# Cross-partition maxima moved from POOL to TensorE products in an attention, gating and feed-forward kernel with a planned instruction order

## The chip, the cores and the metric

The kernel runs on one core of a Trainium2 chip. The metric is device time in microseconds (us), the median of several executions. Five engines run their own instruction lists and meet only at semaphores: PE (TensorE, matrix products), DVE (VectorE), ACT (ScalarE), POOL (GpSimd) and SP (SyncE, which here issues nearly all the DMAs). An engine runs its list strictly in the order in which it was written, so an instruction that waits holds up all that stand behind it, and a DMA that waits in SP's list holds up every later DMA of that list.

## The reference

Three stages follow one another. Attention has 4 batches of 12 heads, with 448 positions of 64 elements:

```
q_n, k_n = rmsnorm(q, g_q), rmsnorm(k, g_k)
scores = scale * q_n @ k_n^T;  attn = softmax(scores);  x = attn @ v
```

Then come a gated block (d_model 768, d_ff 1024) and a feed-forward block with a residual:

```
h = relu(x @ w_in);  u, v = halves of h
v_s = w_spatial (over positions) @ layernorm(v) + b_spatial
x = (u * v_s) @ w_out
out = x + relu(layernorm(x) * g_ln @ w_ch1) @ w_ch2
```

All activations are float32. The weights arrive as 64-bit floats, which the kernel unpacks itself.

## The kernel before

Every large product is done in two-part half precision: a float32 operand is scaled by a power of two and split into a high and a low f16 part (`split`), and three of the four part products are added in PSUM. The scales must be the same on all 128 partitions, so for each operand a bound over all partitions is needed. Most operands get theirs in `sum_scale`: it squares, casts to bf16, multiplies by a matrix of ones on PE, which leaves the sum over partitions in every partition, and derives the power of two with a few narrow DVE instructions. Two bounds are taken in another way: for the batches 1 to 3 of `v` (`v_scale`), and for the maximum of `g_ln`. These call POOL's library routine `partition_all_reduce` with the operation max, and `v_scale` then takes a square root on POOL.

**Attention** goes in 24 pairs of heads (6 pairs to a batch). `att_load` loads q and k into a `raw` tile (4 buffers) and v into `vraw`. `att_front` computes the sums of squares for the norm: ACT squares, DVE reduces, POOL raises to the power -1/2 (`rs`, L192, two pairs at once). `att_back` multiplies `raw` by `rs` on DVE (L207), takes the high part on ACT (L209) and the low part on POOL (L210, for pair 0 on DVE), then issues a DMA transpose into `hT` (L213) and two DMA copies that exchange the halves of `hT` (L215). The scores (L247) need both. The tile `qk16` between L209 and L213 has one buffer. Softmax is L258 to L283, and the product with v is L300 to L307.

**Weights.** `moe1_weights` loads w_in (parts v and u), w_spatial and w_out. `load_weight` fetches 64-bit words into a tile `wide` (2 buffers; the tiles called `v_w`, `u_w`, `o_w` and `r_w` in the trace), and DVE puts the float32 together with three instructions (L422 to L424). The last of the three frees the buffer for the next fetch. `v_scale` fetches a batch of v in three tiles `vpre`, which share two buffers with the squares of `att_front`.

**The gated block** (`moe1`, L543 to L620) of batch b runs beside the attention of batch b+1. Its output goes to DRAM (`x2d`), is read back, normed and transposed into `xnT` (`layernorm`). **The feed-forward block** (`moe2`, L668 and L687) then takes 12 blocks of 256 hidden units, whose weights `prep_block` unpacks.

**The order.** The program is first traced in the order of the Python code, where `merge` interleaves generators: at each step it resumes the one that has used the smallest share of its total, by the numbers that the generators yield. Then `issue_order` throws that order away: `traced` collects the dependences and the rotation of tile buffers, which stays that of the trace; `schedule` runs a model of the machine with costs from `hold`, forward and backward in turns; and `SHAKES` lists how often, and with which random disturbances of the priorities. The last forward pass fixes the order of every engine's list, SP's included. So a change in any cost, in the trace order or in `SHAKES` moves instructions everywhere.

Of the kernel before, what the change touches and what calls it, by code (L numbers as in the profile page):

```python
# [20 lines left out]
P = 128  # L21
# [109 lines left out]
def v_scale(c, b):  # L131


# [16 lines left out]
    if b:  # L150
        am = c.small.tile([P, 1], F32, tag="vam", name=f"vam{b}")
        nc.gpsimd.partition_all_reduce(am[:], mx[:], channels=P, reduce_op=bass_isa.ReduceOp.max)
        nc.gpsimd.tensor_tensor(am, am, c.half, op=ALU.pow)
        c.sv[b] = c.const.tile([P, 2], F32, tag=f"sv{b}", name=f"sv{b}")
        pow2_scale(c, am[:], 14, c.sv[b][:, 0:1], c.sv[b][:, 1:2])
    else:
        nc.vector.tensor_tensor(mx, mx, mx, op=ALU.mult)
        c.sv[b] = sum_scale(c, mx, f"V{b}", pool=c.const)
# [269 lines left out]
def split_weight(c, src, k, n, parts, wide, key):  # L428

    w = c.w1pool.tile([P, 2, k, n], F16, tag=f"w_{key}", name=f"w_{key}")  # L430
    mx = c.small.tile([P, parts], F32, tag="wmx", name=f"wmx_{key}")
    kk = k // parts
    raws = []
    for j in range(parts):
        raws.append(load_weight(c, src[j * kk * P:(j + 1) * kk * P], (kk, n), wide, "wf", f"{key}{j}"))
        squares(c, raws[j], w[:, 1, j * kk:(j + 1) * kk], mx[:, j:j + 1])
        yield 0
    sc = sum_scale(c, mx, key, pool=c.const)
    for j in range(k):
        split(c, raws[j // kk][:, j % kk], w[:, 0, j], w[:, 1, j], sc[:, 0:1])  # L440
        yield 0
    c.w[key] = (w, sc)


def prep_sp(c):
# [6 lines left out]
    for j in range(2):  # L452
# [5 lines left out]
        yield 0  # L458
    sc = sum_scale(c, mx, "sp", pool=c.const)
    for t in range(NTB):  # L460
# [6 lines left out]
        yield 0  # L467
# [239 lines left out]
SHAKES = ((0, 0, 4), (1003, 1000, 3), (1005, 8000, 4), (1012, 8000, 2))  # L707
# [147 lines left out]
def schedule(g, prio, back=False):  # L855
# [18 lines left out]
    for _ in g.ops:  # L874
        best = (math.inf, 0)
        for e, l in todo.items():
            for o in l:
# [3 lines left out]
                if o.xfer > 1000:  # L881
                    s = max(s, dma_at - o.lead)
# [73 lines left out]
def kernel(ctx: ExitStack, tc: tile.TileContext, q, k, v, g_q, g_k, w_in, w_spatial, b_spatial,  # L956
# [43 lines left out]
    c.half = c.const.tile([P, 1], F32, name="half")  # L1000
    nc.vector.memset(c.half, 0.5)
# [15 lines left out]
    gm = c.small.tile([P, 1], F32, tag="gm0", name="gm0", bufs=1)  # L1017
    nc.vector.tensor_reduce(gm, c.gln, axis=AX.X, op=ALU.max, apply_absolute_value=True)
    nc.gpsimd.partition_all_reduce(c.gmax[:], gm[:], channels=P, reduce_op=bass_isa.ReduceOp.max)
    c.gmax2 = c.const.tile([P, 1], F32, name="gmax2")  # L1020
    nc.vector.tensor_tensor(c.gmax2, c.gmax, c.gmax, op=ALU.mult)
# [8 lines left out]
    merge((att(0, 7), 6 * 7000), (moe1_weights(c), 20))  # L1030
# [80 lines left out]
```

## Time and profile before

| | us |
|---|---|
| median of 3 executions (1199.38 to 1205.27) | 1202.64 |
| the profiled execution | 1199.02 |
| its span, first to last instruction | 1197.2 |
| PE busy | 1087.7 (91%) |
| DVE busy | 867.8 (72%) |
| ACT busy | 564.3 (47%) |
| POOL busy | 231.9 (19%) |

The page divides the span into 40 slices of about 30 us. In the first, PE is at 0 tenths; from about 550 us on, in the feed-forward block, it is at 9 tenths throughout. Between the two lie attention and the gated blocks. A busy share is a mean: a stage can be limited by waits that the share doesn't show, so the views that matter here are the stretches (busy time by stage) and the timelines of single engines with the idle time ahead of an instruction.

### The profile page before, as it was taken

The numbers are of one execution on the slowest core, as the hardware profiler recorded it, in microseconds if no ns is written. First come the engines' busy times: TensorE is split into PE (matmuls) and PEld (weight loads), VectorE is DVE, ScalarE is ACT, GpSimd is POOL, SyncE is SP. The second block draws the span as 40 slices with busy tenths as digits, with TensorE's granted clock in tenths as the row PEclk, the third lists the DMA queues.
The fourth block names the chain that finished last, engine by engine and source line by source line (L and its number), as shares of the span: only waits on it lengthen the run. The fifth ranks groups of instructions, "written<-read, shape, count | busy, mean of one in ns | idle before, by whom it ended". The sixth has DMA issues, their size and how long they took to land.

```text
span 1197.2 us, 17032 instructions
## 1 busy us (share of the span) xinstructions
PE 1087.7 (91%) x6385; PEld 570.2 (48%) x6385; DVE 867.8 (72%) x1712; ACT 564.3 (47%) x1088; POOL 231.9 (19%) x166
## 2 busy tenths in 40 slices
PE   0378789799979988997999999999999999999998
PEld 0234335344434434443555555555555555565555
DVE  6778799888897884985985756757584947675334
ACT  2589898678777863656223232414141332313111
POOL 3055458463573320311000000000000000000000
PEclk9989979989989998998999999999999999999999
DMA  8677798999999995888530303111121203010013
GB/s 253 183 193 176 186 204 199 184 212 195 181 206 207 173 159 157 216 199 207 206 106 1 106 1 106 46 61 39 67 75 33 87 20 106 7 48 1 1 53 132
DMA packets 231747, 149.42 MB, mean 125 GB/s; under 512 B 192816, under 2 KB 209264, under 8 KB 231664
## 3 DMA queue, kind: packets, MB, share of 16 engines
q1 hardware_dynamic: 227280, 137.32, 47.7%
q10 hardware_dynamic: 4384, 11.01, 2.7%
q8 instruction: 50, 0.82, 0.3%
q14 instruction: 33, 0.27, 0.1%
HBM read 85.45 MB, written 11.01 MB: 81 GB/s over the span
## 4 chain that ended last, share of the span: by engine, by line
PE 68%; DVE 7%; ACT 5%; DMA 4%; issue 2%; POOL 2%; ACTq 0%; SPq 0%; DVEq 0%; POOLq 0%
PE ps L668 27%; PE ps L687 26%; PE psu L564 4%; PE psv L543 2%; PE ps_o L307 2%; PE ps_s L247 2%; PE pss L577 2%; DMA x2d<-x2o 2%; DVE p L283 2%; ACT pexp L263 1%; PE pso L605 1%; DVE nb L258 1%; POOL rs L192 1%; DMA hT<-qk 1%; ACT p L282 1%
## 5 line engine op out<-in xcount | busy, mean ns | idle before, releaser
L687 PE MATMUL ps<-xnT,wt 128*128 128x384 f16 (+1 forms) x1728 | 347.0, 354 | 8.0 <-DMA xnT<-xn 8.0
L668 PE MATMUL ps<-wt,h 128*128 128x384 f16 x2016 | 344.1, 326 | 0.0
L671 DVE SCALAR_TENSOR_TENSOR x<-ps,wio,x 128x384 f32<-128x384 f32 x336 | 200.6, 614 | 131.6 <-PE ps L668 128.9
L668 PEld LDWEIGHTS <-h 128*128 128x128 f16 x2016 | 196.7, 98 | 133.7 <-issue 0.3
L687 PEld LDWEIGHTS <-wt 128*128 128x128 f16 x1728 | 168.6, 98 | 161.9 <-DMA xnT<-xn 8.5
L690 ACT ACTIVATE hf<-ps 128x512 f32<-128x512 f32 (+1 forms) x96 | 51.9, 540 | 354.1 <-PE ps L687 338.4
L247 PE MATMUL ps_s<-hT 128*64 128x448 f16 x672 | 100.4, 385 | 33.4 <-ACT pexp L263 25.7
L263 ACT ACTIVATE pexp<-ps_s,nb 128x448 f32<-128x448 f32 x168 | 105.5, 639 | 25.9 <-DVE nb L258 22.8
L692 DVE TENSOR_TENSOR h<-hf,h 128x512 f16<-128x512 f32 (+1 forms) x96 | 59.5, 620 | 62.6 <-ACT h L691 62.1
L258 DVE TENSOR_REDUCE nb<-ps_s 128x2 f32<-128x896 f32 x96 | 91.8, 966 | 17.5 <-PE ps_s L247 17.2
L247 PEld LDWEIGHTS <-hT 128*64 128x64 f16 x672 | 39.5, 114 | 126.0 <-issue 53.9
L283 DVE SCALAR_TENSOR_TENSOR p<-pexp,p 128x896 f16<-128x896 f32 x72 | 77.8, 1088 | 15.9 <-ACT p L282 15.5
L282 ACT ACTIVATE p<-pexp 128x896 f16<-128x896 f32 x72 | 61.0, 857 | 6.7 <-DMA pT<-p 5.4
L543 PE MATMUL psv<-w_v,xT 128*128 128x512 f16 (+1 forms) x360 | 64.1, 344 | 0.0
L393 ACT ACTIVATE wt<-r_f 128x1536 bf16<-128x1536 f32 x24 | 35.4, 1477 | 59.4 <-PE ps L668 50.5
L192 POOL TENSOR_TENSOR rs<-ss,mhalf 128x28 f32<-128x28 f32 (+1 forms) x12 | 58.4, 4865 | 15.6 <-DVE ss L189 15.5
L564 PE MATMUL psu<-xT,w_u 128*128 128x448 f16 x288 | 60.9, 358 | 0.0
L210 POOL TENSOR_TENSOR qk<-raw,qk 128x896 f16<-128x896 f32 x23 | 45.5, 1978 | 65.2 <-ACT qk L209 49.3
L691 ACT ACTIVATE h<-hf 128x512 f16<-128x512 f32 (+1 forms) x96 | 55.0, 574 | 2.5
L423 DVE SCALAR_TENSOR_TENSOR r_f<-r_w,r_f 128x256 int32<-128x256 int32 (+1 forms) x96 | 53.2, 555 | 1.3
L424 DVE SCALAR_TENSOR_TENSOR r_f<-r_w,r_f 128x256 int32<-128x256 int32 (+1 forms) x96 | 52.9, 552 | 1.1
L605 PE MATMUL pso<-w_o,g 128*128 128x384 f16 x288 | 51.6, 329 | 2.3 <-ACT g L591 1.4
(193 smaller groups left out, 1240.0 us busy)
## 6 DMA issues: line engine op xcount, KB each, us to landing
r_w<-in_moe_w_ch_dram SPq DMA_DIRECT2D x48, 768.0 KB, 4.4
raw<-in_q_dram SPq DMA_DIRECT2D x24, 224.0 KB, 3.3
raw<-in_k_dram SPq DMA_DIRECT2D x24, 224.0 KB, 3.1
vraw<-in_v_dram SPq DMA_DIRECT2D x24, 224.0 KB, 3.8
vpre<-in_v_dram SPq DMA_DIRECT2D x12, 448.0 KB, 5.4
hT<-hT SPq DMA_DIRECT2D x48, 112.0 KB, 3.0
x<-x2d ACTq DMA_DIRECT2D x14, 384.0 KB, 5.1
out_dram<-x SPq DMA_DIRECT2D x14, 384.0 KB, 2.3
```

What stands on the lines that cost most here:

```text
L192: nc.gpsimd.tensor_tensor(rs, ss, c.mhalf[:, 0:14 * m], op=ALU.pow)
L247: nc.tensor.matmul(ps[hd * 64:hd * 64 + 64, :S], p.hT[:, blk, hd * 64:hd * 64 + 64], kt[:, :, hd * 64:hd * 64 + 64], start=(t == 0), stop= ...
L258: nc.vector.tensor_reduce(nb[:, 0:n], ps[:, 0:n, :S], axis=AX.X, op=ALU.max, negate=True)
L263: nc.scalar.activation(pe[:, j, :], ps[:, j, :S], AF.Exp, bias=nb[:, j:j + 1], scale=1.0, accum_out=p.sm[:, blk:blk + 1])
L282: nc.scalar.activation(p16[:, 0:n, 0], x, AF.Copy, scale=2.0 ** 14)
L283: nc.vector.scalar_tensor_tensor(p16[:, 0:n, 1], x, 2.0 ** 14, p16[:, 0:n, 0], op0=ALU.mult, op1=ALU.subtract)
L543: nc.tensor.matmul(ps[m * h:m * h + m, 0:hn], xT[:, k, x, t * P:t * P + m], wv[:, w, k, h * hn:(h + 1) * hn], start=(n == 0), stop=(n == l ...
L564: nc.tensor.matmul(ps[:, :S], wu[:, w, k, f * P:(f + 1) * P], xT[:, k, x, :], start=(n == 0), stop=(n == len(mms) - 1))
L605: nc.tensor.matmul(ps[:, 0:384], g16[:, f, g, s0:s0 + m], wo[:, w, f, e * 384:(e + 1) * 384], start=(n == 0), stop=(n == len(mms) - 1))
L668: nc.tensor.matmul(ps[:, 0:384], h16[:, f, h, t * P:(t + 1) * P], w2[:, w, f, e * 384:(e + 1) * 384], start=(i == 0), stop=(i == len(mms) ...
L671: nc.vector.scalar_tensor_tensor(xs, ps[:, 0:384], io[:, 0:1], xs, op0=ALU.mult, op1=ALU.add)
L687: nc.tensor.matmul(ps[:, 0:nn], w1[:, w, d, f * P:(f + 1) * P], xnT[:, a:a + n, x * NC6 + d, :], start=(i == 0), stop=(i == len(mms) - 1))
```

## The change

1. `v_scale` no longer calls the library on POOL for the batches 1 to 3. All batches end in `sum_scale`. The batches 1 to 3 pass the sum of squares, which is summed over partitions.
2. The maximum of `g_ln` is replaced by the sum of its squares, summed over partitions by a product with ones (L1014 of the new kernel).
3. The generators of the first weights yield 1 instead of 0, and their total is 32 (the number of their steps) instead of 20. With 0, `merge` resumed them until they were done, directly behind the first step of attention; now they are traced spread over the seven first pairs.
4. In the model of `schedule`, a DMA with a transfer time over 400 (was 1000) may not start before the modelled end of the transfers ahead of it less 1975 (was less its own lead time).
5. `SHAKES` has other seeds, spreads and counts of passes.

```
 def v_scale(c, b):
 ...
     mx = c.small.tile([P, 1], F32, tag="vmx", name=f"vmx{b}")
     nc.vector.tensor_reduce(mx, parts, axis=AX.X, op=ALU.add if b else ALU.max)
-    if b:
-        am = c.small.tile([P, 1], F32, tag="vam", name=f"vam{b}")
-        nc.gpsimd.partition_all_reduce(am[:], mx[:], channels=P, reduce_op=bass_isa.ReduceOp.max)
-        nc.gpsimd.tensor_tensor(am, am, c.half, op=ALU.pow)
-        c.sv[b] = c.const.tile([P, 2], F32, tag=f"sv{b}", name=f"sv{b}")
-        pow2_scale(c, am[:], 14, c.sv[b][:, 0:1], c.sv[b][:, 1:2])
-    else:
+    if not b:
         nc.vector.tensor_tensor(mx, mx, mx, op=ALU.mult)
-        c.sv[b] = sum_scale(c, mx, f"V{b}", pool=c.const)
+    c.sv[b] = sum_scale(c, mx, f"V{b}", pool=c.const)
     yield 0
 ...
 # split_weight (two places) and prep_sp (two places)
-        yield 0
+        yield 1
 ...
-SHAKES = ((0, 0, 4), (1003, 1000, 3), (1005, 8000, 4), (1012, 8000, 2))
+SHAKES = ((0, 0, 4), (1003, 1000, 3), (1033, 20000, 2), (1069, 1000, 3), (1161, 20000, 1))
 ...
 # schedule
-                if o.xfer > 1000:
-                    s = max(s, dma_at - o.lead)
+                if o.xfer > 400:
+                    s = max(s, dma_at - 1975)
 ...
-    c.half = c.const.tile([P, 1], F32, name="half")
-    nc.vector.memset(c.half, 0.5)
 ...
-    gm = c.small.tile([P, 1], F32, tag="gm0", name="gm0", bufs=1)
-    nc.vector.tensor_reduce(gm, c.gln, axis=AX.X, op=ALU.max, apply_absolute_value=True)
-    nc.gpsimd.partition_all_reduce(c.gmax[:], gm[:], channels=P, reduce_op=bass_isa.ReduceOp.max)
+    gm = c.small.tile([P, NC6], F32, tag="gm0", name="gm0", bufs=1)
+    nc.vector.tensor_tensor(gm, c.gln, c.gln, op=ALU.mult)
+    nc.vector.tensor_reduce(c.gmax, gm, axis=AX.X, op=ALU.add)
+    gb = c.small.tile([P, 1], BF16, tag="gb0", name="gb0", bufs=1)
+    nc.vector.tensor_copy(gb, c.gmax)
+    ps = c.ps_x.tile([P, 512], F32, tag="ps_x", name="ps_gm")
+    nc.tensor.matmul(ps[:, 0:1], c.ones, gb, start=True, stop=True)
     c.gmax2 = c.const.tile([P, 1], F32, name="gmax2")
-    nc.vector.tensor_tensor(c.gmax2, c.gmax, c.gmax, op=ALU.mult)
+    nc.vector.tensor_copy(c.gmax2, ps[:, 0:1])
 ...
-    merge((att(0, 7), 6 * 7000), (moe1_weights(c), 20))
+    merge((att(0, 7), 6 * 7000), (moe1_weights(c), 32))
```

The lists of POOL show the removed calls. This is POOL's list before, from the norm of the pairs 1 and 2 on (`rs_189`) to the low part of pair 2; the rows called ISA without a tile are not arithmetic: they change POOL's configuration, once ahead of a library call and once ahead of the ordinary instruction that follows it.

```order
L192 TENSOR_TENSOR rs_189<-ss_179,mhalf 128x28
L1019 ISA
L1019 ISA gmax<-gm_224 128x1
L196 ISA
L196 TENSOR_SCALAR rs_189<-rs_189,qa 128x2x7
L210 TENSOR_TENSOR qk_1_238<-raw_167,qk_1_238 128x14x64
L152 ISA
L152 ISA vam_573<-vmx_571 128x1
L210 ISA
L210 TENSOR_TENSOR qk_2_583<-raw_173,qk_2_583 128x14x64
```

The same piece of POOL's list now (`rs_187` is the norm of the pairs 1 and 2; lines of the new file):

```order
L185 TENSOR_TENSOR rs_187<-ss_177,mhalf 128x28
L189 TENSOR_SCALAR rs_187<-rs_187,qa 128x2x7
L181 TENSOR_TENSOR raw_213<-raw_213,gg 128x448
L203 TENSOR_TENSOR qk_1_240<-raw_165,qk_1_240 128x14x64
L181 TENSOR_TENSOR raw_233<-raw_233,gg 128x448
L203 TENSOR_TENSOR qk_2_409<-raw_171,qk_2_409 128x14x64
```

No ISA row is left between `rs` and the low parts, and two products with the gain (L181) have moved ahead of low parts.

SP's list around the first transpose, before (`v_w_287` is the sixth fetch of w_in, `qk_0` the split q and k of pair 0):

```order
L142 DMA vpre_2_199<-in_v_dram 128x896
L142 DMA vpre_0_562<-in_v_dram 128x896
L418 DMA v_w_287<-in_moe_w_in_dram 128x1024
L213 DMA_TRANSPOSE hT_163<-qk_0_160 128x14x128
L418 DMA u_w_320<-in_moe_w_in_dram 128x1024
L215 DMA hT_163<-hT_163 64x896 x2
```

And now (`v_w_347` and `v_w_352` are the fifth and the sixth fetch of w_in, `vpre_0_387` to `vpre_2_393` those of batch 1 of v):

```order
L411 DMA v_w_347<-in_moe_w_in_dram 128x1024
L141 DMA vpre_0_387<-in_v_dram 128x896
L411 DMA v_w_352<-in_moe_w_in_dram 128x1024
L141 DMA vpre_1_390<-in_v_dram 128x896
L164 DMA vraw_114<-in_v_dram 64x2x448
L206 DMA_TRANSPOSE hT_161<-qk_0_158 128x14x128
L141 DMA vpre_2_393<-in_v_dram 128x896
L165 DMA vraw_114<-in_v_dram 64x2x384
L208 DMA hT_161<-hT_161 64x896 x2
```

The fetch that stood directly ahead of the first transpose now stands three rows ahead of it, and a load of v stands between the transpose and the two copies.

DVE's list before, behind the split of pair 0, whose last instruction (L210, `qk_0`) stands eight rows above the first of these (`raw_167` and `raw_173` are the pairs 1 and 2):

```order
L422 TENSOR_SCALAR v_f<-v_w_275 128x512
L1021 TENSOR_TENSOR gmax_227<-gmax 128x1
L423 SCALAR_TENSOR_TENSOR v_f<-v_w_275,v_f 128x512
L207 TENSOR_TENSOR raw_167<-raw_167,rs_189 128x896
L424 SCALAR_TENSOR_TENSOR v_f<-v_w_275,v_f 128x512
L422 TENSOR_SCALAR v_f<-v_w_282 128x512
L207 TENSOR_TENSOR raw_173<-raw_173,rs_189 128x896
```

And now, up to the split of pair 0 (`raw_111`, `qk_0`); the products of the pairs 1 and 2 with `rs` (L200) stand a few rows above the first of these:

```order
L417 SCALAR_TENSOR_TENSOR v_f<-v_w_292,v_f 128x512
L104 SCALAR_TENSOR_TENSOR rs_143<-rsq_q_146,rs_143 128x14
L145 TENSOR_REDUCE vparts_190<-vpre_2_197 128x1
L189 TENSOR_SCALAR rs_143<-rs_143,qa 128x7
L148 TENSOR_REDUCE vmx_200<-vparts_190 128x1
L200 TENSOR_TENSOR raw_111<-raw_111,rs_143 128x896
L415 TENSOR_SCALAR v_f<-v_w_347 128x512
L150 TENSOR_TENSOR vmx_200<-vmx_200 128x1
L416 SCALAR_TENSOR_TENSOR v_f<-v_w_347,v_f 128x512
L80 CAST ssb_V_203<-vmx_200 128x1
L203 TENSOR_TENSOR qk_0_158<-raw_111,qk_0_158 128x14x64
```

The split of pair 0 now stands behind the products of the pairs 1 and 2 and behind the last instruction that unpacks `v_w_292`, the one that frees the buffer for `v_w_352`.

## Rows read from the trace of the kernel before

**Rows 1.** Page, part 1: busy time, share of span, instructions.

```profile
PE 1087.7 (91%) x6385; PEld 570.2 (48%) x6385; DVE 867.8 (72%) x1712; ACT 564.3 (47%) x1088; POOL 231.9 (19%) x166
```

**Rows 2.** Stretches: length; busy PE, PEld, DVE, ACT, POOL; clock; DMA share; GB/s.

```profile
0.00:41.00 41.00, 0.00 (x0) 0.10 (x1) 24.92 (x62) 8.54 (x12) 9.43 (x12) 1.00 0.69 210
41.00:240.00 199.00, 162.85 (x929) 74.52 (x928) 171.44 (x283) 163.52 (x350) 104.10 (x65) 0.94 0.87 195
240.00:440.00 200.00, 187.69 (x1229) 88.74 (x1229) 172.09 (x258) 154.05 (x318) 96.50 (x66) 0.95 0.98 192
...
550.00:1197.20 647.20, 642.39 (x3694) 360.54 (x3694) 414.02 (x890) 180.08 (x318) 0.00 (x0) 1.00 0.20 66
```

**Rows 3.** Timeline of PE: start, length, what, and idle time before it.

```profile
42.90 0.96 PE L247 MATMUL ps_s<-hT 128*64 128x448 f16 x4 [1.71 <-DMA hT<-qk]
46.06 2.45 PE L247 MATMUL ps_s<-hT 128*64 128x448 f16 x12 [1.04 <-DMA hT<-hT]
82.78 1.33 PE L247 MATMUL ps_s<-hT 128*64 128x448 f16 x6 [4.90 <-DMA hT<-hT]
148.46 0.57 PE L247 MATMUL ps_s<-hT 128*64 128x448 f16 x4 [4.22 <-ACT pexp L263]
550.60 10.37 PE L687 MATMUL ps<-xnT,wt 128*128 128x384 f16 x48 [8.01 <-DMA xnT<-xn]
```

**Rows 4.** Timeline of SP's DMA issues around the first transpose.

```profile
37.02 0.33 SPq L418 DMA_DIRECT2D v_w<-in_moe_w_in_dram  x1
37.39 2.98 SPq L213 DMA_TRANSPOSE hT<-qk  x1
```

**Rows 5.** Timeline of DVE, the same stretch.

```profile
19.84 1.09 DVE L210 TENSOR_TENSOR qk<-raw,qk 128x896 f16<-128x896 f32 x1 [0.56 <-ACT qk L209]
...
35.29 1.09 DVE L207 TENSOR_TENSOR raw<-raw,rs 128x896 f32<-128x896 f32 x1 [6.45 <-POOL rs L196]
36.30 0.68 DVE L424 SCALAR_TENSOR_TENSOR v_f<-v_w,v_f 128x512 int32<-128x512 int32 x1
```

**Rows 6.** Timeline of POOL around three of its four library calls.

```profile
16.06 4.82 POOL L192 TENSOR_TENSOR rs<-ss,mhalf 128x28 f32<-128x28 f32 x1
27.67 0.38 POOL L1019 PARTITION_ALL_REDUCE gmax<-gm  x1 [6.79 <-DVE v_f L422]
34.98 0.28 POOL L196 TENSOR_SCALAR rs<-rs,qa 128x14 f32<-128x14 f32 x1 [6.93 <-issue]
...
68.89 1.88 POOL L210 TENSOR_TENSOR qk<-raw,qk 128x896 f16<-128x896 f32 x1 [8.70 <-ACT pexp L263]
...
139.52 2.12 POOL L210 TENSOR_TENSOR qk<-raw,qk 128x896 f16<-128x896 f32 x1 [7.05 <-issue]
```

**Rows 7.** Timeline of ACT: two instructions that wait for DMAs.

```profile
9.97 0.95 ACT L186 ACTIVATE sq<-raw 128x896 f32<-128x896 f32 x1 [2.94 <-DMA raw<-in_k_dram]
...
145.75 0.95 ACT L209 ACTIVATE qk<-raw 128x896 f16<-128x896 f32 x1 [3.68 <-DMA hT<-qk]
```

**Rows 8.** Groups, 0 to 45 us: count, busy us, mean ns, idle before.

```profile
L424 DVE SCALAR_TENSOR_TENSOR v_f<-v_w,v_f 128x512 int32<-128x512 int32 x6 | 4.1, 688 | 0.1
...
L207 DVE TENSOR_TENSOR raw<-raw,rs 128x896 f32<-128x896 f32 x3 | 3.3, 1090 | 6.5 <-POOL rs L196 6.5
...
L146 DVE TENSOR_REDUCE vparts<-vpre 128x1 f32<-128x896 f32 x3 | 3.2, 1079 | 0.0
...
L422 DVE TENSOR_SCALAR v_f<-v_w 128x512 int32<-128x512 int32 x6 | 2.5, 423 | 4.2 <-DMA v_w<-in_moe_w_in_dram 4.2
...
L103 DVE SCALAR_TENSOR_TENSOR rsq_q<-rsq_q,ss 128x14 f32<-128x14 f32 x3 | 1.4, 470 | 0.0
...
L189 DVE TENSOR_SCALAR ss<-ss 128x14 f32<-128x14 f32 (+1 forms) x2 | 0.3, 172 | 0.0
```

**Rows 9.** One line: the products with ones; min, median, max ns.

```profile
L83 PE MATMUL pssc<-ssb,ones x24: 163/167/167, 491.9 to 1099.4; 128*128 128x1 bf16 x24
```

**Rows 10.** Page, part 5: DVE unpacking the feed-forward weights.

```profile
L423 DVE SCALAR_TENSOR_TENSOR r_f<-r_w,r_f 128x256 int32<-128x256 int32 (+1 forms) x96 | 53.2, 555 | 1.3
```

More of the change, by code (lines that the diff above doesn't have):

```diff
@@ L6 @@
 import concourse.tile as tile
-from concourse import bass_isa, mybir
+from concourse import mybir
 from concourse.masks import make_identity
@@ L440, in split_weight @@
         split(c, raws[j // kk][:, j % kk], w[:, 0, j], w[:, 1, j], sc[:, 0:1])
-        yield 0
+        yield 1
     c.w[key] = (w, sc)
@@ L457, in prep_sp @@
                 mx[:TB, j:j + 1])
-        yield 0
+        yield 1
     sc = sum_scale(c, mx, "sp", pool=c.const)
@@ L466, in prep_sp @@
         nc.sync.dma_start_transpose(out=spT[:, t], in_=sp16.rearrange("p a k -> p (a k)"))
-        yield 0
+        yield 1
     c.w["sp"] = (spT, sc)
```

## The prediction

> **What bounds the kernel now.** First the page's busy times: PE 1087.7 us of the span of 1197.2 [rows 1], so 109.5 us at most can be won without taking products away, and the change takes none away. Then the stretches, to see where these lie [rows 2]: 41.0 us at the start without a product; 36.2 us between 41 and 240 (199.0 less 162.85); 12.3 us from 240 to 440; 4.9 us behind 550; the rest, 15.2 us, between 440 and 550, of which one wait for `xnT` is 8.01 [rows 3]. Behind 550 PE is full: whatever makes earlier work end sooner there is kept whole. So the question is what ends the start, and what the 36.2 us wait for.
>
> *The start.* The first product of scores comes at 42.90, released by the transpose, the second group at 46.06, released by the copies [rows 3]. The transpose was issued at 37.39 [rows 4]. But its input was finished by DVE at 19.84 + 1.09 = 20.9 [rows 5]. Between these it stood in SP's list behind the fetch `v_w` issued at 37.02 [rows 4], which needs the buffer that DVE frees with L424 at 36.30 + 0.68 = 36.98 [rows 5]. That L424 stands behind a product with `rs` (L207), before which DVE idled 6.45 us for POOL [rows 5], and POOL made `rs` only at 34.98, having idled 6.93 us, released by nothing the profile shows, behind the library call at 27.67; ahead of that call it idled 6.79 more, put down to a DVE instruction [rows 6]. The power itself had ended at 16.06 + 4.82 = 20.9 [rows 6]. So one library call with its two changes of configuration costs POOL 14.1 us (20.9 to 35.0), and through DVE, a buffer and SP's list it holds the first transpose.
>
> *Two later calls.* The low part of pair 2 starts on POOL at 68.89 after 8.70 idle, and PE then waits 4.90 us for that pair's copies (82.78) [rows 6, 3]. The idle time is put down to ACT, but one change of configuration stands there too (the order of POOL). At 139.52 another low part comes after 7.05 us released by nothing shown [rows 6]; its transpose has to leave the single `qk16` buffer, ACT waits 3.68 us for that at 145.75 [rows 7], and PE waits 4.22 us for ACT at 148.46 [rows 3].
>
> **The change part by part.**
>
> *Library calls gone.* Four calls, three small powers and eight changes of configuration leave POOL. In their place come four products with ones of 0.16 us on PE [rows 9] and four or five more narrow DVE instructions of 0.17 us [rows 8], below 2 us in all and spread; at nothing, since DVE is idle 27.6 us of the stretch from 41 to 240 [rows 2]. Without that cover they would cost these 2 us.
>
> The Trainium skill speaks against this part: "GPSIMD Engine Reference", section "4.1 Engine selection", sends a reduction over partitions to GPSIMD. By it the call would be the cheap form and its replacement a loss; the row has 0.38 us for the call itself but 14.1 us from `rs` to `rs`, against 0.16 us for the product, so the trace disagrees, and the sum goes by the rows.
>
> *The start anew.* I follow the new lists with durations of before.
> - SP: the k of pair 0 now stands eighth. By the shapes 1475 KB are issued up to it; before, 1472 KB were issued up to the k of pair 1, for which ACT waited until 9.97 [rows 7]. So ACT starts the three squares at 10.0 and ends at 10.0 + 3 x 0.95 = 12.9; DVE's third reduction over 128x896 ends 1.08 later, at 13.9 [rows 7, 8].
> - DVE then has 35 instructions up to the split of pair 0: 4 of 0.423, 7 of 0.688, 3 reductions of 1.079, 4 products of 1.09, and 17 narrow ones of 0.172 [rows 8]: 1.7 + 4.8 + 3.2 + 4.4 + 2.9 = 17.0. End: 30.9. POOL's `rs`, 14.7 + 4.8 [rows 6], is there at 20, before DVE comes to it, and the high part on ACT (about 0.95) lies under the 1.4 us of unpacking between.
> - SP: the five rows ahead of the transpose wait for buffers that DVE frees ahead of that split, so they are out by then. The transpose goes at 30.9 rather than 37.39, and with the same 5.5 us to the first product [rows 3, 4] PE starts at 36.4 rather than 42.90. The copies now have loads of 640 KB ahead of them where 512 KB stood before; I leave their 3.2 us. Gain 6.5.
> - Bounds: narrow instructions were 0.47 in the mean where they met POOL's work [rows 8]: 17 x 0.3 = 5.1 later, gain 1.4. If the transpose finds empty queues and narrow instructions overlap, some 2.5 sooner, gain 9.
>
> The first work behind it is pushed in front too: pairs 1 and 2 are multiplied before pair 0, so their transposes follow quickly, where before pair 2 came at 82.78.
>
> *The later calls.* Pair 2: 4.9 us of PE's wait, between 0 (ACT was really late) and 4.9. Call of batch 2: 4.2, between 0 and 4.2. Call of batch 3: PE had products of the gated block then; 1, between 0 and 3. I take 4, 4 and 1, near the upper ends, because the releasers stand in the rows. What is late next there is DVE: 171.4 busy of 199.0, and ACT with 163.5 [rows 2].
>
> *Weights spread, order anew.* All the same work is done, so this has no price of its own; it moves work of ACT and DVE from the first pairs to later ones, where PE is fuller. In the new lists some 10 us less of DVE's and ACT's work stands before the scores of pair 12 (counted with these durations). At best it takes 10 us off the stretch up to 240, where they are the fullest engines; at worst it costs as much behind 240, where PE has 12.3 us idle and the DMA share is already 0.98 [rows 2]. I take a gain of 3. The weights keep their slack: w_o is split at pair 7 in both lists and used at pair 12.
>
> *The changed model* costs nothing by itself. It can only show as an order.
>
> *Sum.* 6.5 + 4 + 4 + 1 + 3 = 18.5 on PE's start and waits. The stretch from 41 to 240 would have to end 12 sooner after its start, 187 us for 171.4 of DVE's work, 92% busy rather than 86%: possible, but new orders bring waits of their own; I take 3.5 off. Net 15.0: 1199.0 of the profiled execution becomes 1184. The median of the runs shown lies 3.6 above that execution, so 1202.6 - 15 = 1187.6; I say **1187**. Own range of this case: 1176 (all upper ends: 9 + 4.9 + 4.2 + 3 + 5 = 26) to 1195.
>
> **The rivals.**
>
> *The idle time only moves* (1199, from 1196 to 1203). PE's products are the same, and PE is at 91% where POOL is at 19% [rows 1]. The first product comes 6.5 sooner, but from 41 to 440 the DMA share is 0.87 and 0.98 [rows 2], and the transposes and loads of these pairs end when they ended before, less about 3: 1202.6 - 3. For it: the shares. Against: the DMA share of the first 41 us is 0.69 [rows 2], so there is room ahead, and the waits of PE lead back to POOL. The Trainium skill would have it so: "Perfetto Trace Analysis", section "Identifying the Most-Contended Engine", says to improve the engine with the highest occupancy first, and POOL has the lowest here; by that alone the time would stay at 1202.6. The trace agrees on who is fullest, and disagrees as far as rows 4 to 7 show an engine at 19% holding PE.
>
> *The first transpose is held again* (1195, from 1192 to 1199). One of the five loads ahead of it waits for a late buffer, or a late load keeps DVE; the start stays at 42.9 and only 15 - 6.5 = 8 are left. For it: five loads and a serial list. Against: each wait ends on a DVE instruction that stands ahead of the split itself.
>
> *Slower, at the entry to the feed-forward block* (1210). PE already waits 8.01 us for `xnT` at 550.60 [rows 3]. SP's list has fetches of the second and third block's weights between the last transposes, now as before; they wait for buffers that DVE frees. If DVE, with work pushed behind pair 12, unpacks one block late there, the last transposes wait with it: L423 takes 53.2 us for 96 [rows 10], 4.4 for the 8 of a block; with L424 of the same shape 8.9, and for the third instruction 0.423 to 0.688 of that [rows 8], 2.7: 11.6 us. With none of the earlier gain kept that is 1214, with the start's 6.5 kept 1208; I take 1210. It decides from the point at which the wait grows by more than what is won ahead of it. For it: the wait is there already. Against: the order of these rows is nearly the old one.
>
> **How the numbers follow.** Forecast 0.58, idle time only moves 0.17, transpose held again 0.12, slower 0.13. Less than 0.5% (6 us) can't be told from no change here; faster means below 1196.6. The forecast lies there but for its edge (0.56), held again to about two thirds (0.08), moved idle time to a quarter (0.04), in all 0.68; slower 0.12; the same 0.20. For 8 in 10 the range goes from 1174, a little beyond the upper ends, to 1205, which leaves out the slower case and little else.
>
> **What would show it.** Right: no library call on POOL; the first transpose issued near 31 with DVE never idle for POOL before it; scores from about 36; no idle time of 4 us on PE before the scores of pair 2 and near 148; the feed-forward block starting some 15 us sooner and lasting as long. Wrong: a first transpose behind a fetch that waits, idle time on PE that appears behind 240 in place of the old, or more than 8 us before the first product that needs the last `xnT`.

## The result, and the profile after

The changed kernel takes 1185.5 us (median of 4 runs, 1183.9 to 1188.8) where the kernel before took 1201.4 on the same chip: ratio 0.9868, 95% interval 0.9833 to 0.9902, or 15.9 us less. The profiled execution of it takes 1186.0 us, its span 1184.2. The forecast was 1187.

The page's busy times answer to [rows 1]: no engine has over 4 us more or less to do. The stretches that answer to [rows 2] (same columns) show where PE works earlier.

```profile
PE 1085.6 (92%) x6389; PEld 567.0 (48%) x6389; DVE 864.2 (73%) x1716; ACT 568.0 (48%) x1088; POOL 233.8 (20%) x159
```

```profile
0.00:41.00 41.00, 4.20 (x22) 1.52 (x22) 29.09 (x85) 15.16 (x23) 12.46 (x13) 1.00 0.81 248
41.00:240.00 199.00, 171.75 (x994) 75.37 (x994) 178.02 (x287) 168.15 (x361) 102.20 (x59) 0.96 0.91 200
240.00:440.00 200.00, 180.98 (x1176) 85.98 (x1175) 164.51 (x245) 148.88 (x305) 97.08 (x63) 0.96 0.94 187
440.00:550.00 110.00, 98.33 (x565) 50.09 (x564) 84.16 (x222) 60.67 (x93) 22.09 (x25) 0.97 0.74 199
550.00:1184.20 634.20, 630.31 (x3637) 354.00 (x3635) 408.46 (x880) 175.16 (x310) 0.00 (x0) 1.00 0.19 64
```

PE has 4.2 us of products ahead of 41 where it had none, and 171.75 us between 41 and 240 where it had 162.85. From 240 to 440 it is idle for 19.0 us, against 12.3 before: part of the gain is given back there (the same stretch holds other work now, but the table of pairs below shows the lead fall too, from 22.9 us at pair 19 to 6.1 at pair 23). From 440 to 550 it is idle for 11.7 us, against 15.2.

The granted clock of PE over the whole profiled execution is 0.982 and was 0.973. It can't be the main cause: over the kernels below, the clock does not order the times (medians of their executions: n1 0.975 and 1181.1 us, c1 0.98 and 1202.6).

The start, in the order in which it runs: DVE, POOL, SP's issues and PE (answers to [rows 5, 6, 4, 3]; columns as there).

```profile
11.91 3.19 DVE L180 TENSOR_REDUCE ss<-sq 128x14 f32<-128x896 f32 x3 [0.67 <-ACT sq L179]
...
21.42 1.09 DVE L200 TENSOR_TENSOR raw<-raw,rs 128x896 f32<-128x896 f32 x1
...
28.68 1.09 DVE L203 TENSOR_TENSOR qk<-raw,qk 128x896 f16<-128x896 f32 x1
...
39.50 1.09 DVE L251 TENSOR_REDUCE nb<-ps_s 128x2 f32<-128x896 f32 x1 [0.29 <-PE ps_s L240]
```

```profile
15.81 5.19 POOL L185 TENSOR_TENSOR rs<-ss,mhalf 128x28 f32<-128x28 f32 x1 [0.53 <-DVE ss L182]
21.09 0.30 POOL L189 TENSOR_SCALAR rs<-rs,qa 128x14 f32<-128x14 f32 x1
...
45.21 1.89 POOL L203 TENSOR_TENSOR qk<-raw,qk 128x896 f16<-128x896 f32 x1 [0.36 <-ACT qk L202]
```

```profile
25.29 0.33 SPq L411 DMA_DIRECT2D v_w<-in_moe_w_in_dram  x1
...
29.80 1.63 SPq L206 DMA_TRANSPOSE hT<-qk  x1
...
33.94 1.17 SPq L208 DMA_DIRECT2D hT<-hT  x2
```

```profile
33.92 0.96 PE L240 MATMUL ps_s<-hT 128*64 128x448 f16 x4 [3.26 <-DMA hT<-qk]
37.67 0.16 PE L83 MATMUL pssc_V<-ssb_V,ones 128*128 128x1 bf16 x1 [2.79 <-DVE ssb_V L80]
...
61.97 0.38 PE L240 MATMUL ps_s<-hT 128*64 128x448 f16 x2
...
139.09 3.05 PE L240 MATMUL ps_s<-hT 128*64 128x448 f16 x16 [3.77 <-ACT pexp L256]
```

POOL scales its norm at 21.09, not at 34.98, and DVE takes it up at 21.42 without a wait. The split of pair 0 (L203) ends at 28.68 + 1.09 = 29.77, its transpose goes at 29.80, and the first scores come at 33.92, 9.0 us sooner than at 42.90. The low part of pair 2 comes at 45.21 (68.89 before), and the scores of that pair at 61.97 without a wait. A wait for ACT like that of 4.22 us at 148.46 is still there: 3.77 us at 139.09, four products of scores further on (at the first of pair 7).

The feed-forward block begins like this in PE's timeline, first before, then now (answers to the last of [rows 3]):

```profile
511.41 3.83 PE L687 MATMUL ps<-xnT,wt 128*128 128x512 f16 x17
```

```profile
498.49 4.48 PE L680 MATMUL ps<-xnT,wt 128*128 128x512 f16 x20
...
536.23 6.01 PE L680 MATMUL ps<-xnT,wt 128*128 128x384 f16 x36 [2.26 <-DMA xnT<-xn]
545.16 3.46 PE L680 MATMUL ps<-xnT,wt 128*128 128x384 f16 x12 [2.92 <-DMA xnT<-xn]
```

It begins at 498.49; before it was 511.41, so 12.9 us sooner. The two waits for `xnT`, 2.26 and 2.92 us, are together 5.2, where one of 8.01 stood. From there to the span's end it is 685.7 us, and was 685.8: nothing is won or lost behind.

How the gain runs through the program is seen from the first product of the scores of each pair. These are the times before, and the differences to them in single profiled executions (the kernels behind the first column are those of the experiments below; the last column is the kernel with a call put back, less the changed kernel):

```
pair  before  changed  b4     b3     a1     n1     n2     a2   | c1 less changed
 0     42.9    -9.0   -6.9   +0.3   +1.6  -14.4   +1.3   -6.9  | +15.5
 3     94.1   -19.1   -8.5   -1.7   -5.1  -23.8   -0.8   -9.2  | +16.2
 7    152.1   -13.0  -11.1   -5.4   -8.4  -19.1   -2.9   -4.6  | +15.4
12    240.3   -13.1   -9.4   -3.7   -9.9  -15.8   -0.4   -4.9  | +16.5
19    370.3   -22.9   -7.2   -4.4  -12.9  -25.4   -6.0  +16.8  | +16.8
23    427.6    -6.1   -7.2   -4.4   -6.4   -7.7   +4.9  +15.8  | +16.8
end  1197.2   -13.0   -7.6   -5.7   -7.7  -15.4   +4.3  +15.2  | +16.5
```

Single executions scatter: the twelve of n2 go from 1191.6 to 1204.4 us. The traced one of before, 1199.0, is faster than the medians of that kernel (1201.4 here, 1201.9 to 1203.5 beside the experiments), and the traced one of n2, 1203.3, is 4.9 slower than its own, so the last row shows less gain, or more loss, than the medians. The verdicts below go by the medians.

### The profile page after: what moved, and what is told of

Read it like the earlier page. It is cut to its first block, busy times and chain, and to the rows that moved or that the text cites. A ratio compares the mean times of both kernels' runs of the same rounds, so it can differ in the third digit from the quotient of the medians.

```text
span 1184.2 us, 17022 instructions
## 1 busy us (share of the span) xinstructions
PE 1085.6 (92%) x6389; PEld 567.0 (48%) x6389; DVE 864.2 (73%) x1716; ACT 568.0 (48%) x1088; POOL 233.8 (20%) x159
## 4 chain that ended last, share of the span: by engine, by line
PE 66%; DVE 13%; ACT 7%; issue 5%; POOL 4%; DMA 3%; SPq 1%; ACTq 0%; POOLq 0%; DVEq 0%
PE ps L661 28%; PE ps L680 26%; PE pso L598 3%; DVE nb L251 3%; ACT pexp L256 2%; POOL rs L185 2%; DVE p L276 2%; PE pss L570 2%; PE ps_s L240 2%; PE psu L557 1%; PE ps_o L300 1%; DVE ss L180 1%; ACT p L275 1%; DMA vpre<-in_v_dram 1%; DMA raw<-in_q_dram 1%
## 5 line engine op out<-in xcount | busy, mean ns | idle before, releaser
L680 PE MATMUL ps<-xnT,wt 128*128 128x384 f16 (+1 forms) x1728 | 337.3, 353 | 5.2 <-DMA xnT<-xn 5.2
L661 PE MATMUL ps<-wt,h 128*128 128x384 f16 x2016 | 335.7, 326 | 0.0
L664 DVE SCALAR_TENSOR_TENSOR x<-ps,wio,x 128x384 f32<-128x384 f32 x336 | 203.2, 614 | 127.1 <-PE ps L661 125.8
L276 DVE SCALAR_TENSOR_TENSOR p<-pexp,p 128x896 f16<-128x896 f32 x72 | 76.1, 1059 | 14.3 <-ACT p L275 14.1
L536 PE MATMUL psv<-w_v,xT 128*128 128x512 f16 (+1 forms) x360 | 61.1, 340 | 0.0
L203 POOL TENSOR_TENSOR qk<-raw,qk 128x896 f16<-128x896 f32 x23 | 44.4, 1929 | 59.6 <-ACT qk L202 59.5
```

Source lines behind the costliest of these rows:

```text
L276: nc.vector.scalar_tensor_tensor(p16[:, 0:n, 1], x, 2.0 ** 14, p16[:, 0:n, 0], op0=ALU.mult, op1=ALU.subtract)
L536: nc.tensor.matmul(ps[m * h:m * h + m, 0:hn], xT[:, k, x, t * P:t * P + m], wv[:, w, k, h * hn:(h + 1) * hn], start=(n == 0), stop=(n == l ...
L661: nc.tensor.matmul(ps[:, 0:384], h16[:, f, h, t * P:(t + 1) * P], w2[:, w, f, e * 384:(e + 1) * 384], start=(i == 0), stop=(i == len(mms) ...
L664: nc.vector.scalar_tensor_tensor(xs, ps[:, 0:384], io[:, 0:1], xs, op0=ALU.mult, op1=ALU.add)
L680: nc.tensor.matmul(ps[:, 0:nn], w1[:, w, d, f * P:(f + 1) * P], xnT[:, a:a + n, x * NC6 + d, :], start=(i == 0), stop=(i == len(mms) - 1))
```

## The experiments

Each was timed in five rounds beside the kernel before, whose median there was 1201.9 us (b1 to b4), 1203.5 (a1, a3, n1, c1) or 1203.4 (n2, n3, a2, a5); differences are to that median. Theory A: the four library calls on POOL cost the time, by the waits that the prediction named. Its rivals: the new order brings the gain (B), or SP's list alone holds the start. The parts of the change are numbered as in the section on the change.

```
kernel  what it is                                   us      ratio to before [95%]
b4      before, four calls as copies, same order   1190.7   0.9902 [0.9886, 0.9919]
b3      before, three later calls as copies        1195.1   0.9942 [0.9921, 0.9962]
b1      before, first call behind the scaling      1196.7   0.9950 [0.9930, 0.9969]
b2      before, first transpose ahead of a fetch   1204.7   1.0018 [1.0002, 1.0033]
c1      changed, one idle call, same order         1202.6   0.9990 [0.9974, 1.0005]
a1      parts 1, 2                                 1192.3   0.9906 [0.9884, 0.9929]
a3      parts 1, 2, 3                              1194.6   0.9925 [0.9900, 0.9949]
n3      parts 1, 2, 4                              1188.9   0.9888 [0.9863, 0.9914]
n1      parts 1, 2, 3, 4                           1181.1   0.9813 [0.9790, 0.9835]
n2      parts 1, 2, 3, 5                           1198.4   0.9959 [0.9938, 0.9981]
a5      parts 1, 2, 4, 5                           1181.6   0.9820 [0.9798, 0.9841]
a2      parts 3, 4, 5                              1213.8   1.0081 [1.0061, 1.0101]
        all five (the changed kernel)              1185.5   0.9868 [0.9833, 0.9902]
```

**b4: what the calls cost, with every list as it was.** The same edit is made to `am` and `mx` in `v_scale`; the planner's price for the copies stays that of the calls, so that its lists don't change.

```
-    nc.gpsimd.partition_all_reduce(c.gmax[:], gm[:], channels=P, reduce_op=bass_isa.ReduceOp.max)
+    nc.gpsimd.tensor_scalar(c.gmax, gm, 1.0, 0.0, op0=ALU.mult, op1=ALU.add)
```

> The kernel before, with every list of instructions as it is; each of the four library calls on POOL is replaced by one narrow copy (so the maxima over partitions are left out, and the scales of the batches 1 to 3 and of w_out are those of each partition). Theory A (the calls cost the time): POOL has the norm of the pairs 1 and 2 scaled at about 21.2 instead of 34.98, DVE's idle time of 6.45 us for POOL goes, the first scores come at 36.4 instead of 42.9, the waits of 4.90 us (82.78) and 4.22 us (148.46) on PE shrink below 1.5 us, and the time falls by 10 to 15 us: most of what the change won. Rival B (the new order wins it): the first scores come 6.5 us sooner, but the end falls by 0 to 4 us, since the stretch from 41 to 440 is held by DVE, ACT and the DMAs.

Measured: 11.2 us less. POOL and SP:

```profile
16.05 4.80 POOL L192 TENSOR_TENSOR rs<-ss,mhalf 128x28 f32<-128x28 f32 x1
20.84 0.57 POOL L1022 TENSOR_SCALAR gmax<-gm 128x1 f32<-128x1 f32 x1
21.39 0.98 POOL L196 TENSOR_SCALAR rs<-rs,qa 128x14 f32<-128x14 f32 x1
```

```profile
29.07 0.33 SPq L418 DMA_DIRECT2D v_w<-in_moe_w_in_dram  x1
29.45 3.16 SPq L213 DMA_TRANSPOSE hT<-qk  x1
```

From the norm to its scaling there are 0.5 us where there were 14.1; the transpose goes at 29.45, the scores come at 36.0. PE's two waits (at 72.81 and 138.25 now) are 1.53 and 1.37 us. So theory A holds: without any new order the calls are worth 11 us, some 70% of the whole change.

**b3: the three later calls alone.**

```
-        nc.gpsimd.partition_all_reduce(am[:], mx[:], channels=P, reduce_op=bass_isa.ReduceOp.max)
+        nc.gpsimd.tensor_scalar(am, mx, 1.0, 0.0, op0=ALU.mult, op1=ALU.add)
```

> The kernel before, with every list as it is; only the three later library calls (batches 1 to 3) are narrow copies (their maxima over partitions are left out). Theory A: the start stays (first scores at 42.9), the PE waits of 4.90 us (82.78) and 4.22 us (148.46) go, and the time falls by 5 to 9 us. Rival C (PE's waits there are really for ACT, DVE and transfers): these waits shrink by less than half and the time falls by 0 to 3 us.

Measured: 6.8 us less. These are PE's waits that stood at 82.78 and 148.46, and a third:

```profile
80.19 0.76 PE L247 MATMUL ps_s<-hT 128*64 128x448 f16 x6 [1.76 <-DMA hT<-hT]
...
143.92 0.57 PE L247 MATMUL ps_s<-hT 128*64 128x448 f16 x4 [1.37 <-ACT pexp L263]
...
156.84 0.57 PE L247 MATMUL ps_s<-hT 128*64 128x448 f16 x4 [2.77 <-ACT pexp L263]
```

The first shrinks from 4.90 to 1.76 and the second from 4.22 to 1.37, as theory A has it: by 6.0 us together. The third, 2.77 us for ACT, stood ahead of the same product before, and the calls had no part in it:

```profile
162.48 0.57 PE L247 MATMUL ps_s<-hT 128*64 128x448 f16 x4 [2.67 <-ACT pexp L263]
```

Of the forecast 9 us some 7 are real.

**b1: the first call alone, moved and not removed.** `l` is POOL's finished list; the scaling of the norm stands directly behind the call there.

```
+    k = next(n for n, o in enumerate(l) if type(o.i).__name__ == "InstPartitionAllReduce")
+    l[k], l[k + 1] = l[k + 1], l[k]
```

> The kernel before, all computed and every list as it is but for one swap on POOL: the first library call (for gmax) stands behind the multiplication of the norm of the pairs 1 and 2 instead of ahead of it. Theory A: that multiplication ends at about 21.2, DVE's 6.45 us idle for POOL goes, the sixth fetch of w_in is issued near 30.6 and the first transpose near 31, the first scores come at 36.4; of these 6.5 us 3 to 6.5 reach the end. Rival B: the start gains as much, and the end less than 2 us. If a call in the way isn't what holds the start, the first scores stay within 1.5 us of 42.9.

Measured: 5.2 us less. POOL and SP:

```profile
20.85 0.94 POOL L196 TENSOR_SCALAR rs<-rs,qa 128x14 f32<-128x14 f32 x1
28.53 0.38 POOL L1032 PARTITION_ALL_REDUCE gmax<-gm  x1 [6.74 <-issue]
```

```profile
31.33 0.33 SPq L418 DMA_DIRECT2D v_w<-in_moe_w_in_dram  x1
31.71 2.78 SPq L213 DMA_TRANSPOSE hT<-qk  x1
```

The call is still made, and only its place differs: the transpose goes at 31.71 instead of 37.39, the scores come at 37.2, 5.7 us sooner. So the start was held by the call in the way, as the prediction traced it; b1 and b3 together give 12.0, b4 11.2.

The 5.2 us rest on the medians. The traced execution of b1 (1199.8, where the median is 1196.7) does not keep the gain: against the trace before, its products of scores are 5.7 us sooner at pair 0, 4.8 at pair 3, 0.7 at pair 7, and its end is 0.8 later. The largest part goes between 102 and 113. These are the stretches before and in b1 (columns as in [rows 2]):

```profile
102.00:113.00 11.00, 7.73 (x55) 4.34 (x54) 9.39 (x19) 10.84 (x25) 4.46 (x3) 1.00 0.80 178
```

```profile
102.00:113.00 11.00, 8.79 (x42) 4.26 (x43) 8.34 (x13) 8.09 (x19) 3.02 (x2) 0.69 0.95 234
```

PE had its full clock there before and 0.69 of it in b1 (part of the time at the lower of its two levels, 1.2 GHz): a run of 14 products of scores took 3.10 us instead of 1.78. The idle times of PE just ahead, 1.08 and 0.67 us for ACT, stand in both traces, so these rows don't show why the clock fell. A few us of scatter from one execution to the next, in one and the same order, can come from this.

**b2: only SP's list.** `l` is SP's finished list; `t`, the transpose and the two copies of pair 0, moves ahead of `k`, the sixth fetch of w_in.

```
+    t = [o for o in l if writes(o, "hT0")]
 ...
+    k = next(n for n, o in enumerate(l) if writes(o, "v2_w1"))
 ...
+    rest = [o for o in l if o not in t]
+    k = rest.index(l[k])
+    l[:] = rest[:k] + t + rest[k:]
```

> The kernel before, all computed and every list as it is but for SP's: the transpose and the two copies of pair 0 stand ahead of the sixth fetch of w_in, for whose buffer SP waited. By the step of the prediction in which SP's list alone holds the first transpose, it is issued near 21 to 26 and the first scores come at least 9 us sooner. By the lists of PE and DVE it can't be so: PE's first product, of the scale of v, needs DVE behind its idle time (41.0), and the maxima of the scores stand on DVE's list behind the same idle time; then the first scores come at most 2 us sooner, the first maximum of them (48.09) stays within 1 us, and the time stays within 2 us of before.

Measured: 2.8 us more. SP and PE:

```profile
26.77 4.26 SPq L213 DMA_TRANSPOSE hT<-qk  x1
...
38.63 0.34 SPq L418 DMA_DIRECT2D v_w<-in_moe_w_in_dram  x1
```

```profile
42.64 0.16 PE L83 MATMUL pssc_V<-ssb_V,ones 128*128 128x1 bf16 x1 [42.64 <-DVE ssb_V L80]
42.74 0.96 PE L247 MATMUL ps_s<-hT 128*64 128x448 f16 x4
```

The transpose goes 10.6 us sooner and the scores come 0.2 us sooner: PE's first product, for the scale of v, needs DVE behind its wait for POOL. So the queue that the chain ended in was one of several things held by the same call; freeing it alone gains nothing.

**c1: one idle call put back into the changed kernel, every list as it is.** The planner doesn't see the call; it is put into POOL's finished list between the norm of the pairs 1 and 2 and its scaling, and nothing uses its result.

```
+        nc.gpsimd.partition_all_reduce(x[:], c.mhalf[:, 0:1], channels=P, reduce_op=bass_isa.ReduceOp.max)
```

> The changed kernel, all computed and every list as it is, with one idle library call put into POOL's list between the norm of the pairs 1 and 2 (ends at 21.0) and its scaling (21.09). By the 14.1 us of such a call there, the scaling comes at 35.1, DVE's product with it at 35.4 instead of 21.42, the first transpose near 43.8 and the first scores near 47.9 instead of 33.92: 14 us later, and by the share of three quarters that the swapped call gave at the end, the time rises by 7 to 13 us. Rival B (the start is made good by slack up to 440): it rises by 0 to 5 us.

Measured: 0.9 us less than before, so 0.9990 - 0.9868 = 1.2% or 15 us more than the changed kernel. POOL, then DVE:

```profile
15.68 5.19 POOL L185 TENSOR_TENSOR rs<-ss,mhalf 128x28 f32<-128x28 f32 x1 [0.53 <-DVE ss L182]
29.04 0.38 POOL L1032 PARTITION_ALL_REDUCE idle<-mhalf  x1 [8.17 <-issue]
36.56 0.28 POOL L189 TENSOR_SCALAR rs<-rs,qa 128x14 f32<-128x14 f32 x1 [7.14 <-issue]
```

```profile
36.87 1.09 DVE L200 TENSOR_TENSOR raw<-raw,rs 128x896 f32<-128x896 f32 x1 [15.52 <-POOL rs L189]
```

From the norm's end (20.87) to its scaling there are 15.7 us now, DVE waits 15.52, and the whole program is shifted by 15.5 us at pair 0 and by 16.5 at the end (last column of the table of pairs). The expectation of 7 to 13 was too low: nothing of this delay is made good later. One idle call of 0.38 us undoes the change.

**a1 and a3: the calls out and a new order by the old planner, without and with the spread.** a1 is parts 1 and 2 of the diff; a3 has part 3 too, the edit shown (at four places; and 20 becomes 32 in `merge`):

```
-        yield 0
+        yield 1
```

> The kernel before with the first two parts of the change alone (no library calls, sums over partitions in their place), all computed, order worked out anew by the planner as it was before. Theory A: four copies in the place of the calls, with the order fixed, gave 11.2 us; a planner that knows of no call can only use this: 8 to 14 us less than before, 1188 to 1194. Rival P (what a new order brings is as large as what the calls cost): the time lies outside of that, 1183 to 1187 or 1195 to 1202.

> The first three parts of the change (no library calls, weights traced spread over the pairs), all computed, planner and seeds as before. The prediction's step on the spread weights, a gain of 3 with bounds of -5 and +10: 2 to 6 us below the kernel with the first two parts alone, pair 12 of the scores some 5 us sooner than there and the stretch behind 240 with more idle time on PE. Rival P: the difference to that kernel is as large as a new set of seeds makes it, of either sign.

Measured: a1 11.3 us less than before, as theory A had it; a3 8.9, so the spread gave no gain here. In a1, DVE's split of pair 0 and SP's issues:

```profile
16.79 1.09 DVE L204 TENSOR_TENSOR qk<-raw,qk 128x896 f16<-128x896 f32 x1 [1.01 <-ACT qk L203]
```

```profile
35.02 0.33 SPq L412 DMA_DIRECT2D u_w<-in_moe_w_in_dram  x1
...
37.89 0.33 SPq L412 DMA_DIRECT2D u_w<-in_moe_w_in_dram  x1
38.27 2.36 SPq L207 DMA_TRANSPOSE hT<-qk  x1
```

The split ends at 17.9, and the transpose goes 20.4 us later, behind two fetches that wait for buffers; the first scores come at 44.5, later than before. This is the prediction's rival "the first transpose is held again", in a kernel without calls, and yet it is 11 us faster at the end. (a3 has the same: its split ends at 17.8, the transpose goes at 37.38.)

**n1 and n2: the new rule with the old seeds, and the old rule with the new seeds.** Both are edits of the changed kernel, n1 first.

```
-SHAKES = ((0, 0, 4), (1003, 1000, 3), (1033, 20000, 2), (1069, 1000, 3), (1161, 20000, 1))
+SHAKES = ((0, 0, 4), (1003, 1000, 3), (1005, 8000, 4), (1012, 8000, 2))
```
```
-                if o.xfer > 400:
-                    s = max(s, dma_at - 1975)
+                if o.xfer > 1000:
+                    s = max(s, dma_at - o.lead)
```

> The changed kernel with the seeds, spreads and counts of passes of before (parts 1 to 4 of the change), all computed. If seeds only pick among orders of one quality: within 3 us of the changed kernel, 1183 to 1189. If the seeds were worth as much as the spread weights: 1190 to 1195, since 11 us stay from the calls.

> The changed kernel with the rule for DMAs of before in the planner's model (part 4 left out; no calls, weights spread, new seeds), all computed. With the old seeds this rule parted 1194.6 from 1181.1. Theory D (the rule puts the first transpose ahead of fetches that wait for buffers, and later ones too): SP's transpose of pair 0 stands behind two waiting fetches again and is issued 10 us or more behind the split that feeds it, the first scores come after 40, and the time rises by 6 to 14 us over the changed kernel, to 1191 to 1200. Rival S (it was a lucky order): within 4 us of the changed kernel.

Measured: n1 22.4 us less than before, below what was expected; n2 only 5.0 less, within theory D. The split of pair 0 (DVE) and its transpose (SP) in n2, and the same in n1:

```profile
25.67 1.08 DVE L203 TENSOR_TENSOR qk<-raw,qk 128x896 f16<-128x896 f32 x1
```

```profile
33.76 4.10 SPq L411 DMA_DIRECT2D v_w<-in_moe_w_in_dram  x2
...
38.39 3.14 SPq L206 DMA_TRANSPOSE hT<-qk  x1
```

```profile
23.05 1.08 DVE L203 TENSOR_TENSOR qk<-raw,qk 128x896 f16<-128x896 f32 x1
```

```profile
24.16 1.64 SPq L206 DMA_TRANSPOSE hT<-qk  x1
```

With the old rule the transpose goes 11.6 us behind the end of its split, again behind two waiting fetches, and the first scores come at 44.2; with the new rule it goes in the same moment (23.05 + 1.08 = 24.13, 24.16), and they come at 28.5.

**a2, a5 and n3: one part left out, or two alone.** a2 keeps the calls (parts 3 to 5), a5 leaves out the spread (`yield 0` and 20), n3 is parts 1, 2 and 4. One line of each, a2 and a5 against the changed kernel and n3 against the one before:

```
+        nc.gpsimd.partition_all_reduce(am[:], mx[:], channels=P, reduce_op=bass_isa.ReduceOp.max)
 ...
-        yield 1
+        yield 0
 ...
+                if o.xfer > 400:
+                    s = max(s, dma_at - 1975)
```

> The changed kernel with the four library calls kept (parts 3 to 5 of the change alone), all computed, order worked out with them. Theory A: the calls cost what they cost at a fixed order before, 11 us, and in the first 41 us up to 14: 1194 to 1202. Rival: the planner, which has 8 us in its model for a call, plans around them, and the time stays within 5 us of the changed kernel, 1185 to 1190.

> The changed kernel without the spread of the traced weights (part 3 left out), all computed. The prediction's step, a gain of 3 from the spread with bounds of -5 and +10: the time rises by 2 to 6 us, 1187 to 1192. By the pair with the old planner, where the spread gave nothing (1192.3 to 1194.6): 1181 to 1187.

> The kernel before with two edits: no library calls (parts 1 and 2) and the new rule for DMAs (part 4); weights not spread, seeds as before, all computed. Theory D with theory A: these two carry the change, the first transpose is issued within 2 us of the split that feeds it, the first scores come before 34, and the time is 1179 to 1187. If the spread is needed with the rule: 1187 to 1193.

Measured: a2 is 10.4 us slower than before, beyond both expectations; a5 is 21.8 us faster than before, in the range that followed from a1 and a3 and below the one of the prediction's step; n3 14.5, in the range for the case that the spread is needed. In a2 the planner, knowing of the calls, put the first one where POOL had nothing to do, and the scores start at 36.0; its loss comes between the pairs 12 and 19, where one of the calls lies (at 289.35), but where the order also makes PE wait for ACT (3.90 us at 269.66, 5.60 at 310.73). How much of it is the call was not separated.

Side by side, per part (difference of the ratios; an order found anew is part of each):

```
calls out (1, 2):   -0.98% same order (b4); -0.94% (before to a1); -2.1% (a2 to changed)
spread (3):         +0.2% (a1 to a3); -0.75% (n3 to n1); +0.5% (a5 to changed)
rule (4):           -0.2% (a1 to n3); -1.1% (a3 to n1); -0.9% (n2 to changed)
seeds (5):          +0.3% (a3 to n2); +0.55% (n1 to changed); -0.7% (n3 to a5)
```

The calls have one sign and at least 0.9%; the rule has one sign, though a1 to n3 lies within the intervals; the spread and the seeds have both signs, up to 0.75%: so much a new order can do to this kernel by itself. The rule's effect at the start is the same in all seven kernels with parts 1 and 2: the three without the rule (a1, a3, n2) issue the first transpose 11.6 to 20.4 us behind its split, the four with it (n1, n3, a5 and the changed kernel) within 0.1 us, and by the medians each of these four is faster than each of those three. That this transpose is what makes them faster is not shown: n3 has the earliest scores and is the slowest of the four. The two fastest kernels run are n1 and a5, 1181.1 and 1181.6, each with one part of the change undone. Their intervals touch that of the changed kernel (0.9833 to 0.9902), so that they beat it is likely, not shown; that they beat the kernel before is.

## Why the prediction was right, and where it was not

The time was right, and so was the side. Step by step:

- *The chain at the start* (norm, library call, DVE, a buffer, SP's list, transpose): right. b1 and b4 take the call out of the way and the scores come 5.7 and 6.9 us sooner; c1 puts one in and they come 15.5 later.
- *The size at the start*, 6.5: came out at 9.0, the upper bound. The split ended at 29.77 rather than 30.9: DVE's 35 instructions took 14.7 us, not 17.0, because most start before the one ahead has ended (the product with `rs` at 26.51 takes 1.09, the next instruction starts at 27.52). Their durations alone add up to 17.1, as forecast. The reductions ended 1.2 later than forecast. The lower bound took narrow instructions at 0.47; that mean is one of 1.07 beside two of 0.17, and here they took 0.17. And from there to the first product it took 4.1 us instead of 5.5.
- *The later calls*, 9 in all: mis-sized. b3 measures 6.8. The two waits were booked at 4 and 4 and shrank by 3.1 and 2.9; what is left of them (1.76 and 1.37 us) does not hang on the calls. In the new order a wait of 3.77 us stands close to the second, at 139.09. The row at 82.78 is the second group of pair 2, not its first scores as the prediction reads it at one place: these came at 75.45, and now at 61.97. All four calls were put at 15.5, and b4 has 11.2.
- *The spread weights*, a gain of 3: not borne out. It gave +0.2%, -0.75% and +0.5% in three pairs. Nor did it move work behind pair 12 at a price that can be seen apart. The range's lower end counts 5 us for it, where the text allowed 10.
- *"The changed model costs nothing by itself. It can only show as an order."* This is the step that failed. The order it shows as is worth 0.9% with the seeds of the change (n2), some 11 us. Without the rule SP's list puts the first transpose behind waiting fetches even when no call is left (a1, n2). The prediction read the new list correctly, booked the early transpose as a gain of the missing calls, and did not see that the list came from the rule.
- *3.5 taken off for waits of a new order*: the direction was fair. Beyond the calls' 11.2 the change brought 4.7 us by the medians (0.3%, within the intervals), in which a rule that helps meets seeds that here cost 0.55% against the old ones (n1); 240 to 440 has 6.7 us more idle time on PE, in part the sign of being wrong that the prediction named.

So the mechanism of the calls was right, and that 15 forecast and 15.9 measured agree so closely is luck in part: the sum had 4.3 too much for the calls, 3 for the spread, and nothing for the rule.

*The rivals.* "The idle time only moves" is refuted by c1, where the whole shift reaches the end, and by the medians of b1 (not by its trace). "Held again" did not happen here, but is what the change would be without its rule: n2, 1198.4; the prediction had given it 1195. "Slower at the entry to the feed-forward block" did not come: the waits for `xnT` fell from 8.01 to 5.2.

The Trainium skill's rule to send a reduction over partitions to GPSIMD ("GPSIMD Engine Reference", section "4.1 Engine selection") is set against VectorE there; against a product on TensorE it is not borne out by these runs: a call costs POOL 13 to 16 us, and at a fixed order the four of them cost the kernel 11.

## What to carry to other kernels

Follow a late transfer back past the queue that it stands in: several queues can wait for one slow instruction on the emptiest engine, and freeing the last of them alone gains nothing (b2). Price a scheduler's rule by what its order does to the serial queues, and split an effect "at a fixed order" from "with a new order": pinning the lists and changing one instruction gave clean numbers, while new seeds or another trace order moved the time by up to 0.75% either way. An early first product is no measure of the end between two orders (a1's comes later than before the change and it wins 11 us, n3's comes at 27.0, first of all, and it wins 14), though within one order a delay can go through to the end whole (c1).

## What the runs showed of the hardware

The two idle times around a library call are paid on every call, and not by a fixed amount. Before and in b1, b2, b3, c1 and a2 no call had less than 5.7 us of POOL's idle time ahead of it, nor less than 6.9 behind it. For the first call they were 6.79 and 6.93 before [rows 6], 8.17 and 7.14 in c1, 5.88 and 9.64 in b2, whose POOL row behind the call is the first of these; the second is the third call before, with the idle time ahead of it (the one behind it is the 7.05 of [rows 6]):

```profile
36.60 0.28 POOL L196 TENSOR_SCALAR rs<-rs,qa 128x14 f32<-128x14 f32 x1 [9.64 <-issue]
```

```profile
132.08 0.39 POOL L152 PARTITION_ALL_REDUCE vam<-vmx  x1 [5.92 <-DVE ss L187]
```

The change of configuration itself is short in the trace: before, two records MODIFY_POOL_CONFIG of below 0.01 us stand at 20.86 and 20.89, ahead of the first call, and two of 0.083 us at 28.00 and 28.04, behind it, each pair at the beginning of its idle time. Nor is the idle time behind the call a wait for a transfer of the kernel: in c1 the DMA queues moved nothing in it (the last two columns are DMA share and GB/s).

```profile
29.42:36.56 7.14, 0.00 (x0) 0.00 (x0) 0.00 (x0) 0.00 (x0) 0.00 (x1) 1.00 0.00 0
```

In b2 a transpose was being issued during the long one (26.77 to 31.03). Whether it slowed the call was not tried. The Trainium skill ("GPSIMD Engine Reference", section "2.1 Instruction dispatch") tells of about 6 us for loading code at the first call of a freshly loaded kernel; here such a time lies on both sides of the call, the second being paid by the ordinary instruction that follows.
